# A written order of 1,867 steps, replaced by another one, in a fused HGRN2 attention and SERF MLP kernel

## The chip, the cores and the metric

The kernel runs on one core of one Trainium2 chip. The metric is the device time of one execution in microseconds (us). Engine names in the profile: PE is TensorE (PEld its weight loads), DVE is VectorE, ACT is ScalarE, POOL is GpSimd, SP is SyncE, which here issues most DMAs.

## The reference

Two functions in a row, q, k, v and the gate's logits as (4, 8, 768, 48), weights of 384 x 2048 and 2048 x 384:

```python
f = 1.0 / (1.0 + np.exp(-f_logit))
for t in range(S):
    state = f[:, :, t, :, None] * state + np.einsum('bhd,bhe->bhde', k[:, :, t], v[:, :, t])
    y[:, :, t] = np.einsum('bhd,bhde->bhe', q[:, :, t], state)
x = y.transpose(0, 2, 1, 3).reshape(B * S, H * D)     # 3072 x 384
h = x @ w_in
sp = np.maximum(h, 0.0) + np.log1p(np.exp(-np.abs(h)))
return (h * erf(sp)) @ w_out
```

The weights arrive as float64, two 32-bit words an element.

## The kernel before

**Tiling.** The 3072 tokens are 24 chunks of 128 (g = 0 to 23, each in two halves c of 64) and 12 blocks of 256 (blk). Attention goes by chunks, in the chunked form of the recurrence; the MLP goes by blocks and by four groups of 512 hidden columns (gi). The weights come in 16 pieces, 768 KB each as float64: 8 of w_in, 8 of w_out. VectorE and ACT turn a piece into fp32 in seven steps (`round_step`).

**Order.** The program is one list of tokens, STEPS. `run_steps` goes through it and each token issues its instructions at the end of the queues of its engines; the scheduler changes nothing (`manual_schedule`), so each engine executes its instructions in the order of the list, and waits where another engine's result or a free buffer is missing. A token reads `name numbers engine @ places`: `m4_0_1` is the mask of chunk 4, half 0, row group 1; `c1_3a@11` copies block 1, group 3 by ACT (a; v is VectorE) into slot 11. Places are 15 SBUF slots and the PSUM bank pairs 0 to 3.

The tokens that the text speaks of:

- f, q, k, v, p: loads of gate logits, queries, keys, values and a weight piece, by SP. r: a rounding step. cl, ex, ln, d, e: log decays (d on TensorE, "log sums"), qd, kd: queries and keys times decays (VectorE).
- tq, tk, tx: transposes of qd and kd (TensorE), aq, ak: their copies to SBUF (qA, kT).
- sc: *scores* (TensorE, L593), m: *mask* of the scores (VectorE, L618), four per chunk. ds: *state products* (TensorE, L581), to, ta: totals of the decays, st: state update (VectorE, L557/L558). y: attention rows (TensorE, L644), x/xa/xb/xt: their copies.
- h: hidden columns from plain fp32 (L686, blocks 0 to 2). hf, ht: hidden columns from three f32r parts (L705, blocks 3 to 11). c: copy of h. ae, ax, aw, at, au, ah, am: the activation on ACT and VectorE. ka, kb, kt: h in parts. o, oa, ot: output (L772), plain or by parts. nc, no: fetches of parts of w_out from DRAM, by POOL. ro, so, rh, sh: rows out. ck: the check on the decays, whose flag all engines read at the end. z: matmuls on constants that keep TensorE busy (L443).

Attention's matmuls use a part of TensorE's array (64 x 64 tiles and others), the MLP's the whole.

**One bank pair for three results.** Scores, state products and totals of a chunk lie in one bank pair, side by side, in a single tile:

```python
def scored(g, n=None):
    if g not in scs:
        scs[g] = bank_pair(n)
    t = scs[g]
    w = HP * C
    return (
        t[:, :, 0:w].rearrange("s r (a t) -> s r a t", t=C), t[:, :, w : w + HP * D],
        t[:, 0, w + HP * D : w + HP * D + 2 * HP],
    )
```

`mask` reads the first of them, `add_state` the second.

Of the kernel before, what the change touches and what calls it, by code (L numbers as in the profile page):

```python
# [47 lines left out]
def kernel(  # L82
# [760 lines left out]
    def pads(_):  # L843
# [60 lines left out]
        oa4_2 v12 no4_3@2 kt4_1 oa4_3 ak11a@6 aq11@9 o4_1_1_1 at4_3 nc4_4@7 o4_1_0_1 k12 aw4_3@4
        st20 sc11@3 nc4_5@14 ds11 m10_0_1 sp20a d13@0 st21 ot4_2 e13 m11_0_1 st22 y10_1@2 sp21a
        no4_4@5 m11_1_0 y10_0 sp22a td12 m11_1_1 ot4_3 w12 ms12 v13 xa10 m11_0_0 ka4_2@8@1
        y11_1@0 xb10 y11_0 kb4_2 oa4_4 xa11 w13 oa4_5 kt4_2 o4_2_1_1 o4_2_0_1 xb11 f19@8 xt11
        hf5_0@0 nc5_0@14 xt10 nc5_1@1 no4_5@7 au4_3 ht5_0 td13 hf5_4@2 qd12 ah4_3 f18 cl14 ht5_4
# [357 lines left out]
```

## Time and profile before

| | us |
|---|---|
| runs of the kernel | 569.91, 572.71, 574.5 (median 572.71) |
| the profiled execution: its span | 569.7 |
| TensorE busy | 550.9 (97%) |
| VectorE busy | 470.8 (83%) |
| ACT busy | 413.7 (73%) |
| POOL busy | 107.4 (19%) |

The mean granted clock of TensorE in the profiled execution is 0.994. The profile gives no time for the profiled execution beside its span, from the first to the last instruction. A row of the grouped view reads: line, engine, operation, output<-input, count | busy time, mean duration in ns | idle time of the engine ahead of it, and what ended most of it. A row of the timeline reads: start, duration, engine, line, operation, count. A plain fp32 matmul of the program is executed as two, so counts in the profile are twice those of the program there.

### The profile page before, as it was taken

Reading aid. Unit: us, or ns where it says so; the run is one execution under the profiler, and the core shown is the slowest. Engines: PE = TensorE matmul, PEld = TensorE weight load, DVE = VectorE, ACT = ScalarE, POOL = GpSimd, SP = SyncE. Lnnn points to the kernel's source line nnn. Section 1 sums busy time; section 2 is a strip of 40 time slices with the busy share of each in tenths; the row PEclk is TensorE's granted clock in tenths of the full one; section 3 lists DMA queues with packets and bytes.
Section 4 is the critical chain, followed back from the end, with each engine's and each line's share of the span. In section 5 each row is a group of like instructions: output and inputs, shape, how many; then the busy total and the mean of one; then the engine's idle time right before and its main releaser. Section 6 shows DMA issues by size and latency. Waiting matters only on the chain.

```text
span 569.7 us, 14855 instructions
## 1 busy us (share of the span) xinstructions
PE 550.9 (97%) x6175; PEld 462.7 (81%) x6175; DVE 470.8 (83%) x666; ACT 413.7 (73%) x513; POOL 107.4 (19%) x191
## 2 busy tenths in 40 slices
PE   8889999999999999999999999999999999999995
PEld 7768887756678668789979878989979989799983
DVE  5899999999988588987688999478888598695881
ACT  5877758799897575886986976588875766756860
POOL 1023003000030012014032124031215215110220
PEclk9999999999999999999999998999999999999998
DMA  8896785100563136389745889534887657552671
GB/s 192 214 282 149 218 221 159 56 0 0 108 145 65 23 91 217 130 195 250 138 116 148 214 193 248 121 63 137 216 186 201 175 161 204 121 140 61 172 217 62
DMA packets 155714, 85.59 MB, mean 150 GB/s; under 512 B 132244, under 2 KB 135316, under 8 KB 155640
## 3 DMA queue, kind: packets, MB, share of 16 engines
q1 hardware_dynamic: 139128, 42.68, 32.6%
q0 software_dynamic: 16512, 41.89, 26.2%
q8 instruction: 51, 0.84, 0.6%
q14 instruction: 23, 0.19, 0.1%
HBM read 73.41 MB, written 9.51 MB: 146 GB/s over the span
## 4 chain that ended last, share of the span: by engine, by line
PE 58%; DVE 18%; issue 9%; DMA 7%; ACT 5%; SPq 1%; POOL 1%; DVEq 0%; POOLq 0%; ACTq 0%
PE pair L772 25%; PE pair L705 18%; PE pair L686 5%; DVE e L181 4%; DMA piece<-form_dram 3%; PE pair L644 2%; PE pair L593 2%; PE pair L515 2%; PE pair L581 2%; DVE qA L618 1%; DMA raw_x<-in_moe_w_in_dram 1%; DMA out_dram<-rows 1%; DVE raw_y L351 1%; DVE plain_o L358 1%; PE pair L461 1%
## 5 line engine op out<-in xcount | busy, mean ns | idle before, releaser
L181 DVE SCALAR_TENSOR_TENSOR e<-x,e 128x1024 f32<-128x1024 f32 x96 | 116.8, 1220 | 35.4 <-ACT x L176 25.6
L176 ACT ACTIVATE x<-h,serf_bias 128x1024 f32<-128x1024 f32 x88 | 100.0, 1147 | 30.9 <-DVE e L181 14.1
L772 PE MATMUL pair<-plain_o,h 128*128 128x384 f32 x320 | 110.7, 492 | 0.0
L398 POOL DMA_DIRECT2D piece<-form_dram x96 | 52.2, 546 | 275.1 <-PE pair L772 175.4
L772 PEld LDWEIGHTS pair<-plain_o,h 128*128 128x128 f32 x320 | 58.5, 190 | 36.6 <-DVE h L740 0.9
L290 POOL DMA_DIRECT2D sv<-in_v_dram x84 | 53.7, 652 | 168.7 <-PE pair L644 139.1
L772 PE MATMUL pair<-piece,g 128*128 128x384 f32 x384 | 81.3, 349 | 1.5 <-DMA piece<-form_dram 1.2
L705 PE MATMUL pair<-xT,form_x 128*128 128x256 f32 x432 | 77.8, 288 | 0.0
L705 PE MATMUL pair<-xT,form_i 128*128 128x256 f32 x432 | 74.1, 279 | 0.0
L772 PEld LDWEIGHTS pair<-piece,g 128*128 128x128 f32 x384 | 66.7, 190 | 5.8 <-DMA piece<-form_dram 1.8
L736 ACT ACTIVATE e<-e 128x1024 f32<-128x1024 f32 x48 | 50.4, 1054 | 26.2 <-DVE e L181 25.8
L705 PEld LDWEIGHTS pair<-xT,form_x 128*128 128x128 f32 x432 | 62.4, 188 | 4.4 <-issue 0.8
L686 PE MATMUL pair<-xT,plain_i 128*128 128x256 f32 x288 | 64.8, 381 | 0.2 <-DVE plain_i L358 0.2
L705 PE MATMUL pair<-xT,form_y 128*128 128x256 f32 x432 | 61.6, 281 | 0.0
L686 PEld LDWEIGHTS pair<-xT,plain_i 128*128 128x128 f32 x288 | 54.1, 190 | 9.1 <-issue 0.6
L705 PEld LDWEIGHTS pair<-xT,form_i 128*128 128x128 f32 x432 | 60.9, 188 | 0.0
L740 DVE TENSOR_TENSOR h<-h,e 128x1024 f32<-128x1024 f32 x44 | 53.5, 1220 | 5.4 <-ACT e L736 5.3
L705 PEld LDWEIGHTS pair<-xT,form_y 128*128 128x128 f32 x432 | 56.0, 188 | 0.8
L173 ACT ACTIVATE e<-h 128x1024 f32<-128x1024 f32 x44 | 46.0, 1052 | 13.1 <-DVE h L137 5.7
L618 DVE TENSOR_TENSOR qA<-pair,tri 64x256 f32<-64x256 f32 x96 | 40.5, 422 | 7.0 <-PE pair L593 2.8
L772 PE MATMUL pair<-form_o,g 128*128 128x384 f32 x192 | 39.9, 342 | 0.0
L529 ACT COPY qA<-pair 64x512 f32<-64x512 f32 x48 | 27.8, 578 | 12.6 <-PE pair L515 9.0
(105 smaller groups left out, 766.0 us busy)
## 6 DMA issues: line engine op xcount, KB each, us to landing
piece<-form_dram POOLq DMA_DIRECT2D x96, 384.0 KB, 4.0
raw_y<-in_moe_w_out_dram SPq DMA_DIRECT2D x8, 768.0 KB, 4.5
kn<-in_k_dram SPq DMA_DIRECT2D x24, 192.0 KB, 3.0
vt<-in_v_dram SPq DMA_DIRECT2D x24, 192.0 KB, 4.1
qn<-in_q_dram SPq DMA_DIRECT2D x24, 192.0 KB, 4.0
form_dram<-piece SPq DMA_DIRECT2D x12, 384.0 KB, 3.4
out_dram<-rows SPq DMA_DIRECT2D x11, 384.0 KB, 3.4
sv<-in_v_dram POOLq DMA_DIRECT2D x84, 48.0 KB, 3.3
```

Of the source, the lines that this page charges most:

```text
L173: nc.scalar.activation(out=dst[:], in_=h, func=AF.Exp)
L176: nc.scalar.activation(out=dst[:], in_=h, func=AF.Tanh, bias=serf_bias[:, i : i + 1], scale=SERF_KAB[i][0])
L181: nc.vector.scalar_tensor_tensor(out=e[:], in0=x[:], scalar=SERF_KAB[i][2], in1=e[:], op0=ALU.add, op1=ALU.mult)
L290: nc.gpsimd.dma_start(out=svs[g % NSV][half(1 - r), r, c, :, PAD : PAD + D], in_=v[b, r::2, t0 : t0 + C, :].rearrange("a t d -> t a d"),)
L398: nc.gpsimd.dma_start(out=streams[i, blk, u], in_=form_dram[i, u])
L529: nc.scalar.copy(out=qAs[g][half(r), r].rearrange("p a (c t) -> p a c t", c=2), in_=ps[half(r)])
L618: nc.vector.tensor_tensor(out=to, in0=sc[half(c), r], in1=tri1[half(c)].unsqueeze(1).broadcast_to((C, HP, C)), op=ALU.mult,)
L686: nc.tensor.matmul(hts[blk, gi][:, 2 * i + j, :], lhsT=w[:, kt, j * P : (j + 1) * P], rhs=xTs[blk][:, 0, kt, :], start=(kt == 0), stop=(kt ...
L705: nc.tensor.matmul(hts[blk, gi][:, 2 * i + j, :], lhsT=w[:, kt, j * P : (j + 1) * P], rhs=x[:, kt, :], start=(blk, p) not in begun, stop=True,
L736: nc.scalar.activation(out=e[:], in_=e[:], func=AF.Tanh, scale=SERF_C)
L740: nc.vector.tensor_tensor(out=h, in0=h, in1=es.pop((blk, gi))[:], op=ALU.mult)
L772: nc.tensor.matmul(ots[blk][:, tt, 0:d_model], lhsT=lhs, rhs=rhs, start=("o", blk, tt) not in begun, stop=True, skip_group_check=True,)
```

## The change

STEPS is another list. Apart from the dummy matmuls (27 before, 20 after) it holds the same work, in another order, with other slots and bank pairs. Eleven copies of transposed keys (ak) go from VectorE to ACT, and some copies of hidden columns, states, rows and values change between the two; kernel lines move up by 34 to 36. Four helpers take their slots one at a time, and dummies always go to a bank pair that they name:

```diff
-    def out_c(u, n, n2):
-        streams[u] = [piece(m) for m in (n, n2)]
+    def out_c(u, n):
+        streams[u] = [piece(n)]
         take_c(streams[u][0], out_words(u))
+
+    def out_m(u, n):
+        streams[u].append(piece(n))
+        take_m(streams[u][1], streams[u][0], out_words(u))
...
-    def keep_busy(times, n=None):
-        to = busy[-1]
-        if n is not None:
-            ahead[n] = bank_pair(n)
-            to = ahead[n][:, 0, 0:P]
+    def keep_busy(times, n):
+        ahead[n] = bank_pair(n)
         for _ in range(times):
-            nc.tensor.matmul(to, lhsT=tri[:], rhs=tri[:], start=True, stop=True)
+            nc.tensor.matmul(ahead[n][:, 0, 0:P], lhsT=tri[:], rhs=tri[:], start=True, stop=True)
...
-    def part_a(blk, gi, n, n2):
-        gps_[blk, gi] = [slot(m, "g", F32R) for m in (n, n2)]
+    def part_a(blk, gi, n):
+        gps_[blk, gi] = [slot(n, "g", F32R)]
...
-    def part_b(blk, gi):
+    def part_b(blk, gi, n):
+        gps_[blk, gi].append(slot(n, "g", F32R))
...
-    def project(blk, gi, tt, *more):
+    def project(blk, gi, tt, n=None):
         whole = (blk, gi) not in gps_
-        rows_tile(blk, more[-1] if len(more) == (1 if whole else 2) else None)
+        rows_tile(blk, n)
...
     STEPS = """
-        f1@0 f0 k0 p0 zb0@0 in0 v0 cl1 q0 ex1 cl0 ex0 k1 ln0 z11 d0@1 e0 q1 kd0 r0_0 z4 to0@1 v1
...
+        f0@0 cl0 ex0 ln0 z12@0 d0@0 f1 cl1 ex1 ln1 z1@1 d1@1 ms0 in0 q0 v0 k0 q1 e0 z1@2 to0@2
+        v0_1_1v v0_1_0v e1 qd0 tq0@3 aq0@1 kd0 v1 k1 v0_0_1v v0_0_0v qd1 ta0 ds0 st0 st1 sp1v
...
```

**Chunk 4.** On TensorE, before, state products (L581) follow the scores (L593) of chunk 4 at once; its bank pair is pair_879:

```order
L515 MATMUL pair_836<-ident,kd_93 128x64 x8
L686 MATMUL pair_857<-xT,plain_i_519 128x256 x6
L593 MATMUL pair_879<-qA,kT 64x64 x16
L581 MATMUL pair_879<-vt_84,kd_93 64x48 x16
L686 MATMUL pair_919<-xT,plain_i_519 128x256 x12
```

In the changed kernel (scores now L558, state products L546, plain hidden columns L651) chunk 4 has pair_846 and chunk 5 pair_719:

```order
L651 MATMUL pair_851<-xT,plain_i_584 128x256 x6
L558 MATMUL pair_846<-qA,kT 64x64 x16
L558 MATMUL pair_719<-qA,kT 64x64 x16
L546 MATMUL pair_846<-vt_84,kd_93 64x48 x16
L546 MATMUL pair_719<-vt_85,kd_94 64x48 x8
L426 MATMUL pair_937<-lt,tri_60 64x192 x4
L651 MATMUL pair_851<-xT,plain_i_584 128x256 x6
```

On VectorE in the changed kernel, three masks of chunk 4 (L583) stand among rounding steps of weight piece 5 (plain_i_591), and in the list all three stand ahead of ds4:

```order
L572 COPY Tall<-pair_719 128x4x2
L583 TENSOR_TENSOR qA<-pair_846,tri_60 64x4x64 x2
L303 TENSOR_SCALAR plain_i_591<-plain_i_591 128x2x3x128
L572 COPY Tall<-pair_846 128x4x2
L308 SCALAR_TENSOR_TENSOR plain_i_591<-raw_y_605,plain_i_591 128x768
L312 TENSOR_SCALAR raw_y_605<-plain_i_591 128x2x3x128
L583 TENSOR_TENSOR qA<-pair_846,tri_60 64x4x64
L317 SCALAR_TENSOR_TENSOR raw_y_605<-raw_y_605 128x768
```

Before, all masks of a chunk stand behind its state products in the list. In the built program an instruction that touches a tile waits for the earlier ones of other engines that touch it, so state products of chunk 4 now wait for the third mask of these rows.

**Chunk 7.** On TensorE, before, state products come ahead of the scores (pair_1557):

```order
L772 MATMUL pair_1538<-plain_o_778,h 128x384 x4
L581 MATMUL pair_1557<-vt_85,kd_94 64x48 x16
L593 MATMUL pair_1557<-qA,kT 64x64 x16
L772 MATMUL pair_1295<-plain_o_1042,h 128x384 x4
```

In the changed kernel they come behind them (pair_1483):

```order
L738 MATMUL pair_1326<-plain_o_1293,h 128x384 x4
L558 MATMUL pair_1483<-qA,kT 64x64 x16
L546 MATMUL pair_1483<-vt_85,kd_94 64x48 x16
L426 MATMUL pair_1548<-lt,tri_60 64x192 x4
```

and on VectorE the three masks that stand ahead of ds7 in the list come behind rounding steps of a piece of w_out (plain_o_1354), two passes of the activation (e) and queries times decays (qd):

```order
L317 SCALAR_TENSOR_TENSOR raw_y_1359<-raw_y_1359 128x768
L324 TENSOR_TENSOR plain_o_1354<-raw_y_1359,plain_o_1354 128x768
L147 SCALAR_TENSOR_TENSOR e<-x,e 128x1024
L324 TENSOR_TENSOR plain_o_1354<-raw_y_1355,plain_o_1354 128x768
L449 TENSOR_TENSOR qd<-qn_88,dp_95 128x8x48
L147 SCALAR_TENSOR_TENSOR e<-x,e 128x1024
L583 TENSOR_TENSOR qA<-pair_1483,tri_60 64x4x64 x3
```

The masks moved ahead of the state products of the same chunk at these two places, and at chunks 13, 16, 18 and 23.

More of the change, by code (lines that the diff above doesn't have):

```diff
@@ L904 @@
[L904 to L908, printed above, removed]
-        ex14 hf5_1 kd12 ht5_1 ln14 am4_3 hf5_5 q14 c5_0a@4 tt12 ae5_0@11 hf5_2@0 aw5_0@9 hf5_3
@@ new lines @@
+        h0_5@2 r8_0 sp10a h0_4 c0_2a h1_5@1 h1_4 c1_2a@10 tx6@0 aq6@8 ak6a@13 y4_0@3 y4_1 y5_1@2
+        y5_0 x4a x5a r8_1 w7 w6 ds6@1 q8 td6 v7 p11 f9@1 k8 r9_2 au0_1 sc6 m6_1_1 m6_0_0 r8_2
+        r8_3 r9_3 m6_1_0 ah1_0 ax0_2@4 aw1_1@5 r11_0 r9_4 r9_5 v8 f8 tt6 k7 d7@0 e7 ah0_1
+        ae1_3@13 aw0_0@6 m6_0_1 au1_1 am1_0 r9_6 au0_0 r8_4 kd7 r11_1 r11_2 ax1_3@11 r11_3 r8_5
+        r11_4 r11_5 am0_1 cl8 r8_6 st12 h2_4@3 h2_2@2 h2_3 h2_6@0 h2_5 c2_1a@5 ah1_1 ah0_0
+        c2_2a@14 ae1_2@6 ae0_2@2 at0_2 r11_6 ex8 r10_5 st13 q7 p13 sp12a r13_0 h2_7 h2_1@2 at1_3
@@ new lines @@
+        am1_1 r10_6 qd7 r13_1 am0_0 r13_2 r13_3 h2_0 o1_0_1@3 o1_0_0 o1_1_0 o1_1_1 o0_1_1@1
+        o0_0_0 p12 p15 td7 tt7 p14 k9 aw1_3@4 r12_0 ln8 r15_0 r12_1 r13_4 r12_2 r13_5 r13_6
+        aw0_2@11 aw1_2@9 ax1_2@12 c2_0a@7 r14_0 c2_3a@3 au0_2 at1_2 r12_3 r15_1 r12_4 ms6 ah0_2
+        d8@2 ae2_2@11 e8 y6_1@0 y6_0 tx7@2 ak7a@12 o0_1_0 o0_0_1 r12_5 r15_2 r12_6 au1_2 am0_2
+        ah1_2 am1_2 o1_2_0 kci2 ae0_3@8 ax2_3@9 xa6 aq7@2 sc7@2 au1_3 kd8 r15_3 r14_1 r14_2
+        ah1_3 aw0_3@6 ax0_3@4 r15_4 xb6 r15_5 r14_3 am1_3 r14_4 r14_5 r14_6 at0_3 r15_6 sp13a
@@ new lines @@
+        kci0 qd8 au0_3 m7_0_1 m7_1_1 m7_1_0 ds7 kci1 ax2_2@12 d9@0 aw2_2@1 kci3 ae2_3@13 st14
+        st15 m7_0_0 at2_3 f11@4 td8 f10 o1_2_1 o0_2_1 ah0_3 am0_3 aw2_3@10 o0_2_0 kci5 sp14a e9
+        td9 v9 o1_3_0 o1_3_1 ro1a@6 ae2_1@9 ae2_0@0 so1 tt9 q10 tt8 k10 q9 au2_3 kMi0 kMi2 kMi1
+        cl10 kDi1 y7_0@2 y7_1 xa7 xb7 ah2_3 kci4 kDi0 kMi3 xt6 xt7 kDi3 tx8@0 o0_3_0 ax2_0@8
+        ex10 ln10 kco0@2 o0_3_1 kci7 ro0a@10 aw2_1@6 hf3_1@3 hf3_0 ht3_0 at2_2 kd9 qd9 kDi2
+        hf3_3@2 ht3_3 ht3_1 hf3_2 am2_3 o2_3_1@1 ht3_2 o2_3_0 aw2_0@12 at2_0 au2_0 au2_2
@@ new lines @@
+        sc10@0 ds10 td11 q12 k12 sCo4 q11 k11 tt10 sCo2 so0 ro2a@12 so2 w10 w11 d12@1 e12 kDi6
+        kDi5 hf3_5 xb8 hf4_1@3 hf3_4 ht3_7@1 xt8 kDi7 hf3_7 ht4_1 m10_1_0 m10_0_1 ae3_0@7 at3_0
+        m10_1_1 ht3_6 ah3_1 kd11 c3_2v@9 sp19a aw3_2@10 ax3_2@14 qd11 st20 am3_1 kd12 hf3_6
+        ht4_0 m10_0_0 au3_0 st21 sp21v sp20a y10_1@2 y10_0 c3_3a@12 ae3_2@11 at3_2 kMo2@0 au3_2
+        k13 sCo3 v12 td12 q13 tt12 v11 ah3_0 ah3_2 xa10 tx11@1 am3_0 sMo2 kMo3@3 sMo3 k14 tt11
+        ae3_3@14 kco1@10 o3_1_1@0 hf4_0 o3_1_0 am3_2 kDo3 xb10 kco5@7 qd12 ax3_3@11 at3_3
@@ new lines @@
+        nc4_2@4 st27 ax4_1@0 aw4_1@9 ae4_1@2 c5_0v@13 sp26 td15 q15 td14 tt14 tx14@3 ak14a@7
+        aq14@8 y12_0@2 y12_1 xa12 at4_1 kd15 au4_1 y13_1@1 y13_0 xa13 xb13 xb12 ae5_1@14 aw5_1@0
+        at5_1 au5_1 ah4_1 am4_1 aw5_0@10 ah5_1 am5_1 sc14@3 ds14 nc4_3@7 w14 no5_3@9 ot4_0
+        ht5_7@1 hf5_5@2 ht5_5 o4_3_0 ka4_1@6 oa4_2 m14_1_1 kb4_1@5 kt4_1 oa4_3 ht5_6 o4_1_0
+        hf5_7 o4_1_1 no4_1@0 no4_3@2 ot4_3 ot4_1 no4_2@14 ka5_1@4 kb5_1@7 st28 qd15 m14_1_0
+        ax5_0@6 ae5_0@5 kt5_1 m14_0_0 at5_0 hf5_4 ht5_4 c5_2a@2 ae5_2@0 ax5_2@3 au5_0 aw5_2@6
@@ new lines @@
+        ah5_0 hf5_6 ot4_2 o4_3_1 nc5_3@10 no5_2@1 nc5_2@14 q17 sp27 st29 m14_0_1 k16 sp28
+        y14_1@2 tt15 q16 ro4a@11 y14_0 xa14 c5_3a@8 at5_2 xt12 f16@3 k17 so4 f17 v15 sp29 tx15@3
+        ot5_3@0 oa5_3 o5_1_0 hf6_3@1 xt13 am5_0 xb14 au5_2 ax5_3@5 ka5_0@9 kb5_0@10 ah5_2 am5_2
+        kt5_0 ae5_3@6 aw5_3@11 at5_3 au5_3 aq15@0 ka5_2@5 ht6_1@2 oa5_2 o5_1_1 ht6_0 ht6_2 w16
+        hf6_0 hf6_2 ot5_2 kb5_2@4 o5_2_1 o5_0_0 nc5_4@14 oa5_4 ht6_3 ah5_3 xt14 no5_1@7 ot5_1
+        w15 nc5_0@11 hf6_1 o5_2_0 nc5_1@1 no5_4@12 no5_0@14 kt5_2 am5_3 cl16 oa5_0 ex16 ln16
@@ new lines @@
+        ak15a@6 c6_1v@7 c6_0a@4 aw6_0@11 sc15@1 ds15 m15_0_1 st30 st31 d16@3 d17@2 sp30 f18@6
+        ot5_0 ot5_4 o5_0_1 oa5_1 e16 e17 kd17 kd16 qd16 m15_1_1 m15_1_0 o5_3_0 y15_1@3 m15_0_0
+        y15_0 tx16@2 ae6_0@3 ax6_0@13 at6_0 ae6_1@14 ax6_1@12 at6_1 aw6_1@10 au6_1 o5_3_1
+        ht6_4@1 hf6_4 ht6_5 no5_5@1 nc6_3@9 nc5_5@0 ot5_5 oa5_5 hf6_5 nc6_0@13 nc6_2@12 aq16@10
+        ah6_1 au6_0 ah6_0 ak16a@8 q18 k18 td16 f19 am6_1 ka6_1@11 am6_0 xa15 ka6_0@14 oa6_3@2
+        kb6_1@1 o6_1_1 ro5v@2 c6_2a@3 aw6_2@0 kt6_1 qd17 cl18 kb6_0@5 xb15 ht6_6@0 v16 k19 tt16
@@ new lines @@
+        so5 td17 sp31 o6_1_0 oa6_2 hf6_7 sc16@1 m16_0_1 ds16 m16_0_0 kt6_0 st32 st33 tx17@3
+        m16_1_0 tt17 v17 sp32 o6_0_1 ht6_7 oa6_0 o6_0_0 nc6_1@9 oa6_1 hf6_6 ex18 ae6_2@1 ln18
+        ax6_2@11 at6_2 m16_1_1 xt15 aq17@12 ak17a@2 sc17@3 c6_3a@8 ds17 m17_0_0 au6_2 m17_1_1
+        st34 m17_0_1 d18@1 ax6_3@13 e18 ae6_3@5 at6_3 ah6_2 am6_2 kd18 qd18 aw6_3@9 au6_3 ah6_3
+        m17_1_0 am6_3 ht7_2@0 no6_0@14 no6_1@11 w17 no6_3@2 no6_2@0 hf7_3 ht7_1@1 ht7_0 ot6_0
+        ht7_3 hf7_2 c7_1v@13 hf7_1 ot6_1 tx18@3 ak18a@14 aq18@1 hf7_0 c7_0a@9 ax7_0@4 ot6_2
@@ new lines @@
+        sc18@0 m18_1_0 m18_0_0 td18 sp34 q19 sp33 v18 v19 tt18 ds18 m18_1_1 st36 st37 ot6_3
+        y17_1@3 m18_0_1 k20 f21@11 f20 ae7_0@5 at7_0 ax7_1@0 y16_0@1 y17_0 aw7_1@14 xa17 ms18
+        xb17 y16_1 ae7_1@2 d19@0 e19 o6_3_1 ht7_6@3 o6_3_0 ht7_4@0 kd19 xa16 xb16 qd19 cl20
+        ka6_2@7 ex20 ln20 at7_1 au7_1 kb6_2@12 kt6_2 nc6_4@10 tx19@1 oa6_4 hf7_7 hf7_6 w18
+        no6_5@6 no6_4@4 ot6_4 ht7_7 no7_2@0 nc6_5@8 oa6_5 ot6_5 ah7_1 am7_1 aw7_0@14 au7_0
+        aq19@10 c7_3v@2 ah7_0 am7_0 ka7_1@4 ht7_5 o6_2_0 o6_2_1 kb7_1@14 xt16 ak19a@7 ro6a@8
@@ new lines @@
+        au10_0 ah9_3 ah10_0 am10_0 ka10_0@12 aw10_2@0 at10_2 au10_2 kb10_0@8 ht11_1@0 ot9_4
+        hf10_3 ot9_5 hf10_6 ht10_2 c10_1v@7 ax10_1@9 nc10_0@14 no9_2@10 nc10_4@5 no10_2@0 ht11_0
+        hf10_7 ht10_7 hf11_0 ck0 o10_0_0@1 oa10_1 o10_0_1 oa10_0 ot9_2 am9_3 o9_3_1 o9_3_0
+        ae10_1@2 ah10_2 at10_1 c10_3v@4 am10_2 ka10_2@14 oa10_4 nc10_3@9 kb10_2@3 o10_2_0
+        o10_2_1 ht11_7@2 ht11_6 nc10_5@10 aw10_1@13 ro9a@11 so9 au10_1 ah10_1 am10_1 ax10_3@13
+        ae10_3@5 at10_3 ka10_1@2 kb10_1@11 ht11_2@3 ht11_3 oa10_5 hf11_1 c11_0a@13 ax11_0@10
@@ new lines @@
+        kt10_2 kt10_1 kt10_0 ae11_0@3 oa10_3 o10_1_1 ht11_4@0 ot10_2 hf11_2 o10_1_0 hf11_3
+        no10_5@14 ot10_5 no10_3@9 ot10_3 hf11_6 hf11_7 nc10_2@8 oa10_2 no10_4@12 ot10_4 hf11_4
+        aw11_0@0 at11_0 au11_0 aw10_3@10 ah11_0 au10_3 ah10_3 am11_0 am10_3 no10_0@11 ka11_0@0
+        kb11_0@10 c11_1v@14 ae11_1@7 aw11_1@9 ot10_0 nc11_0@3 oa11_0@3 no11_0@5 no10_1@2
+        nc11_1@8 c11_3v@6 ax11_3@12 kt11_0 ot11_0 ax11_1@11 at11_1 au11_1 aw11_3@3 ae11_3@5
+        at11_3 au11_3 ht11_5 hf11_5 c11_2a@11 aw11_2@9 ah11_3 am11_3 ah11_1 am11_1 oa11_1 ot10_1
@@ L989 @@
+        o10_3_0 o10_3_1 ro10v@0 so10 o11_3_0 no11_1@8 nc11_2@1 ot11_1 ax11_2@2 nc11_5@12
+        nc11_3@3 ka11_1@5 ae11_2@4 kb11_1@7 o11_1_1 o11_0_1 oa11_3 oa11_2 o11_3_1 o11_1_0 at11_2
+        au11_2 ah11_2 am11_2 kt11_1 ka11_2@8 kb11_2@13 kt11_2 no11_2@2 ot11_2 o11_2_1 oa11_5
+        no11_3@0 no11_5@9 ot11_5 nc11_4@3 ot11_3 oa11_4 no11_4@1 ot11_4 rh11_1v@4 sh11_1 o11_2_0
+        o11_0_0 rh11_0a sh11_0 ck1@2 ck2
     """.split()
@@ L992, in run_steps @@
         do = {
-            "z": keep_busy, "zb": lambda _, n: busy.append(bank_pair(n)[:, 0, 0:P]), "f": load_f, "p": load_piece, "r": round_step, "w": load_sv, "in": pads,
+            "z": keep_busy, "f": load_f, "p": load_piece, "r": round_step, "w": load_sv, "in": pads,
             "q": lambda g: load(g, q, qns[g % NQ]), "k": lambda g: load(g, k, kns[g % NQ]), "v": load_v,
@@ L1005, in run_steps @@
             "nc": fetch_form(0), "no": fetch_form(1), "oa": project_form(0), "ot": project_form(1),
-            "kco": out_c, "kMo": lambda u: take_m(streams[u][1], streams[u][0], out_words(u)),
+            "kco": out_c, "kMo": out_m,
             "kDo": out_d, "sCo": keep_form(0), "sMo": keep_form(1),
```

197 lines of the change are left out of this document (64 added, 133 removed).

## The prediction

> **What bounds the kernel now.** I read the page first (busy time, the slices), then the stretches of 20 us, then TensorE's and VectorE's own rows, and last the waits.
>
> ```profile
> span 569.7 us, 14855 instructions
> PE 550.9 (97%) x6175; PEld 462.7 (81%) x6175; DVE 470.8 (83%) x666; ACT 413.7 (73%) x513; POOL 107.4 (19%) x191
> 0.00:20.00 20.00, 16.02 (x212) 14.27 (x212) 13.53 (x33) 12.93 (x27) 1.74 (x11) 1.00 0.89 204
> 20.00:40.00 20.00, 17.78 (x367) 14.11 (x358) 17.67 (x41) 15.14 (x34) 3.33 (x5) 1.00 0.98 266
> 40.00:60.00 20.00, 18.85 (x176) 16.26 (x175) 19.89 (x32) 16.01 (x19) 5.99 (x7) 1.00 0.64 142
> 100.00:120.00 20.00, 20.00 (x82) 15.16 (x81) 20.00 (x24) 16.29 (x18) 0.00 (x0) 1.00 0.13 40
> 120.00:140.00 20.00, 19.66 (x65) 11.92 (x64) 20.00 (x22) 19.87 (x21) 0.00 (x0) 1.00 0.00 0
> 340.00:360.00 20.00, 18.42 (x257) 16.34 (x256) 15.45 (x25) 10.39 (x16) 7.61 (x14) 0.91 1.03 235
> ```
>
> The columns behind the length are busy time of PE, PEld, DVE, ACT, POOL, then granted clock, DMA share and GB/s. TensorE is busy 97% of the whole, but that is an average of two regimes. From 40 to 140 us VectorE has no gap either (19.89 to 20.00 of 20 in the rows shown): it turns the float64 weights into fp32 (the rounding steps), and TensorE keeps pace with it. Afterwards (row 340) VectorE has slack and TensorE alone sets the pace. So the first 140 us are decided by how the two queues interlock, the rest by TensorE's work and its few waits.
>
> A busy TensorE hides its losses, because ends of matmuls are modelled. So I count work from start to start.
>
> ```profile
> 43.60 18.37 PE L686 MATMUL pair<-xT,plain_i 128*128 128x256 f32 x84 [0.20 <-DVE plain_i L358]
> 61.90 0.88 PE L461 MATMUL pair<-lt,tri 64*64 64x192 f32 x16
> 62.71 2.86 PE L686 MATMUL pair<-xT,plain_i 128*128 128x256 f32 x12
> 65.50 0.47 PE L515 MATMUL pair<-ident,qd 64*128 64x64 f32 x8
> 65.80 0.41 PE L515 MATMUL pair<-ident,kd 64*128 64x64 f32 x8
> 66.14 2.86 PE L686 MATMUL pair<-xT,plain_i 128*128 128x256 f32 x12
> 68.93 0.69 PE L593 MATMUL pair<-qA,kT 48*64 48x64 f32 x32
> 69.44 0.63 PE L581 MATMUL pair<-vt,kd 64*64 64x48 f32 x32
> 70.01 5.45 PE L686 MATMUL pair<-xT,plain_i 128*128 128x256 f32 x24
> 86.94 2.01 PE L644 MATMUL pair<-qA,sv 128*32 128x64 f32 x128
> 88.88 5.43 PE L772 MATMUL pair<-plain_o,h_x 128*128 128x384 f32 x16
> 94.14 6.21 PE L686 MATMUL pair<-xT,plain_i 128*128 128x256 f32 x28
> ```
>
> ```profile
> 394.90 0.86 PE L772 MATMUL pair<-piece,g 128*128 128x384 f32 x4
> 395.60 0.87 PE L705 MATMUL pair<-xT,form_y 128*128 128x256 f32 x6
> 397.71 0.52 PE L705 MATMUL pair<-xT,form_x 128*128 128x256 f32 x3
> 398.06 0.52 PE L705 MATMUL pair<-xT,form_i 128*128 128x256 f32 x3
> ```
>
> A plain hidden record takes (61.90 - 43.60) / 84 = .218 us (a plain fp32 matmul is two records), scores .51 / 32 = .016, state products .57 / 32 = .018, attention rows 1.94 / 128 = .015, transposes .34 / 8 = .043, log sums .81 / 16 = .05, plain output 5.26 / 16 = .329 (the mean over the whole trace is .31), output by parts .70 / 4 = .175, hidden by parts .35 / 3 = .118.
>
> ```profile
> 101.45 0.54 DVE L333 TENSOR_SCALAR plain_o<-plain_o 128x768 f32<-128x768 f32 x1
> 101.92 0.94 DVE L351 SCALAR_TENSOR_TENSOR raw_y<-raw_y 128x768 f32<-128x768 uint32 x1
> 102.79 1.21 DVE L740 TENSOR_TENSOR h_x<-h_x,e 128x1024 f32<-128x1024 f32 x1
> 103.92 0.94 DVE L358 TENSOR_TENSOR plain_o<-raw_y,plain_o 128x768 f32<-128x768 f32 x1
> L618 DVE TENSOR_TENSOR qA<-pair,tri 64x256 f32<-64x256 f32 x96 | 40.5, 422 | 7.0 <-PE pair L593 2.8 <-PE pair L581 2.5
> ```
>
> VectorE likewise, start to start: one-input rounding step .47, two-input step .87, a pass over 1024 columns 1.13 to 1.14, a mask .42. The mask's row also says that masks (L618) waited 2.5 us for *state products* (L581), which they do not read: the two share a bank pair, and the program orders whoever touches it.
>
> **The change, part by part.** *Changes between whole-array and part tiles.* In the built order 46 excursions into part tiles stand where 65 stood. One costs about .2: 12 hidden records between two excursions take 2.79, against 12 x .218 = 2.61. 19 x .2 is about 4 us of TensorE, all on its path from 140 us on. Without that saving the sum below is 4 higher (rival C). Seven dummy matmuls fewer (27 to 20) lie in waits of the start and give nothing.
>
> *Fetches.* Two visible waits on form pieces go, since the new list asks earlier:
>
> ```profile
> PE pair L772 <- DMA piece<-form_dram: 1.2, 2, 1.0
> PEld pair L772 <- DMA piece<-form_dram: 1.8, 2, 1.2
> ```
>
> I credit 1.6, between these rows' 1.2 and 1.8.
>
> *Engines.* Eleven kT copies go to ACT, other copies change sides: VectorE's work falls by some 11 us, ACT's rises by 8. VectorE is saturated only before 140 us, where few of these lie.
>
> *The new wait.* In six chunks (4, 7, 13, 16, 18, 23) state products now stand behind masks of the same chunk; before, none did. Two of them lie where VectorE is saturated. State products of chunk 4 are matmuls after 54.9 us of TensorE's work, but wait for a mask that ends after 58.6 us of VectorE's. I count VectorE's list to there: 22 two-input steps 19.3, 24 one-input 11.6, 19 masks 8.0, 12 decays 5.6, 15 state updates 4.7, the rest 9.4. VectorE's own idle time comes on top. Before, it is 6.5 in the first 20 us and 2.3 in the next (20 - 13.53, 20 - 17.67). The new list loads gates, queries and values ahead of the weights, so I take 5.5, bounds 4 and 8.9. TensorE then stands at 58.6 + 5.5 = **64.1**. Queued behind it is everything on TensorE: its own loss so far would be about 4, so 5 us are new.
>
> Next, mask 6 on VectorE waits for scores 6. From state products 4, TensorE has 84 plain hidden records 18.2, attention rows 2.0, state products and scores 1.8, transposes and log sums 1.1: **23.1**. VectorE has 16.0 in the same stretch, so it goes idle for 7.1 us with its rounding queued behind the mask.
>
> Then state products 7, after 46.6 us more of TensorE, wait for three masks. VectorE has 23 two-input steps 20.0, 18 one-input 8.4, 17 wide passes 19.4, 7 masks 3.0, the rest 4.2: **55.0**. TensorE waits 8.4 us. So the path crosses over three times, each time to the engine with more in hand.
>
> *Clock.* The trace has one stretch at half clock:
>
> ```profile
> 349.24 0.21 PE L515 MATMUL pair<-ident,qd 64*128 64x64 f32 x1 [1.28 <-issue]
> 351.02 2.81 PE L772 MATMUL pair<-piece,g 128*128 128x384 f32 x8
> 353.62 1.31 PE L772 MATMUL pair<-form_o,g 128*128 128x384 f32 x4
> 354.77 0.52 PE L705 MATMUL pair<-xT,form_x 128*128 128x256 f32 x3
> ```
>
> After a wait of 1.28, twelve matmuls took 3.75 where 12 x .175 is 2.1: 1.65 lost (the row 340:360 says .91 of 20, 1.8). I take 1.4 behind each of the two long waits, bounds 0 and 3.4, as part of the slow time may fall into the wait. The Trainium skill ("TensorE: Matmul & The Clock Gate", What's actually happening) lets the clock fall to half after an idle window of about 3.4 us and rise again after a busy window as long. By it both long waits bring half clock, an estimate of up to 1.7 lost behind each, and the sum would be .6 higher at most; the wait of 1.28 above, shorter than its window, would have brought none, and there the trace disagrees.
>
> *The other four chunks*, where VectorE has slack: scores, one to three masks of .42, at 23 also a copy of 1.1 ahead, then state products: .7 to 2 us each, 5 together. Scores 9 and 11 now stand behind state updates of the same pair (.36 each for two steps and more): 1.5. At the end the copy of one half of the last rows stands ahead of the other half's last matmuls: .8. With small change, 7.5; bounds 5 and 10.
>
> *TensorE's rest* after state products 7: 312 plain output records 96.6 (at .31), 576 by parts 101.7, 1296 hidden by parts 153.3, attention rows 17.4, scores and state products 16.6, transposes 10.3, log sums 6.4: **402.4**.
>
> *What is lost anyway.* The same counting for before leaves 16.3 us between 162 and 563.2: six single waits of 4.9 (1.2 of them the fetches), half clock 1.4, and 10 in many small hand-overs. I keep 10 (8.5 to 11) and 1 for clock.
>
> *The end.*
>
> ```profile
> 561.75 1.45 PE L772 MATMUL pair<-plain_o,h 128*128 128x384 f32 x4
> 563.24 0.56 DVE L137 COPY rows<-pair 128x384 f32<-128x384 f32 x1 [6.26 <-PE pair L772]
> 563.82 0.90 SPq L816 DMA_DIRECT2D out_dram<-rows  x2
> 563.88 0.48 ACT L137 COPY rows<-pair 128x384 f32<-128x384 f32 x1 [8.16 <-DVE rows L137]
> ```
>
> From 563.2 to 569.7 are 6.5. After, one of the copies is done earlier (-.5), but the last steps of the check on the decays now come last: 6.8.
>
> *Sum:* 64.1 + 23.1 + 1.4 + .4 (scores and first mask) + 55.0 = 144.0 at state products 7; + 1.4 + 402.4 + 10 + 7.5 + 1 + 6.8 = **573.1**, against the profiled 569.7: **+3.4**. The median of the runs shown, 572.71, lies 3.0 above that span (the lowest, 569.91, .2 above). So I say **576**.
>
> **The rivals.**
> *A, faster: the masks hold nobody up.* For it: it needs no more than VectorE being earlier, or the waits being met. Then TensorE's list of 124.6 + 402.4 = 527.0, some 4 lost early, 2.3 at mask 6, 10 + 2.3 + 1 and 6.8 give 553.4, a run of 556. If only VectorE's own list binds (129.6 + 5.5 = 135.1 at state products 7, no idle time at mask 6), 564.2, a run of 567. Against: TensorE executes in order, and the built program has these waits.
>
> *B, slower: VectorE is late by ACT too.* In the third stretch ten of the 17 wide passes are e<-x,e, which need ACT's terms:
>
> ```profile
> L181 DVE SCALAR_TENSOR_TENSOR e<-x,e 128x1024 f32<-128x1024 f32 x96 | 116.8, 1220 | 35.4 <-ACT x L176 25.6 <-ACT e L173 8.9
> ```
>
> 35.4 / 96 is .37 each, 3.7 for ten; all of it is on the path, because TensorE already waits for VectorE there. It decides from the point where ACT delivers later than VectorE arrives. With it 576.8, a run of 580; with the high start (8.9 idle) 583. Against: the row 100:140 had no idle VectorE.
>
> *C, the saving isn't there:* excursions cost only what the neighbours give back; then 4 us come back, a run of 580. Against: the 2.79 above, for a gap of its own.
>
> **How the numbers follow.** Forecast .50 (own range 569 to 582), A .28 (two thirds at 556 to 562, the rest near 567), B .14, C .08. Within 1% (567.0 to 578.4, about what a measurement here can tell from no change): .42, nearly all of it the forecast's. Faster by more: .27. Slower by more: .31 (B, C, and the upper part of the forecast, where the start is late or w is 10). Range 558 to 585: down into A, up to B with a late start; each end leaves about a tenth.
>
> **What would show it.** State products of chunk 4 starting near 64 us with an idle TensorE of about 5 ahead, released by VectorE's mask; VectorE idle for 7 us ahead of a mask near 80 to 88; TensorE idle for about 8 near 144; half clock in the two stretches behind; no wait on form pieces above .3; some 4 us less from start to start over the rest. I am wrong if these three waits are short: then the time is A's. I am wrong upward if further waits of several us show behind ACT between 90 and 144.

## The result, and the profile after

The changed kernel takes 589.67 us (median of four runs, 587.21 to 591.0), against 573.61 of the kernel before in the same runs: a ratio of 1.0295, interval 1.0238 to 1.0352. It is slower by 16 us; forecast were 3.4, in a range that ended at 585. Here and below a median takes in every run, while a ratio leaves out runs far above the rest of the same kernel (of the kernel before one of 577.52, of the last two versions one each, of 2779.56 and 1892.95).

The profiled execution has a span of 589.3 us. Page and stretches of 20 us, columns as before:

```profile
span 589.3 us, 14768 instructions
PE 551.1 (94%) x6161; PEld 466.7 (79%) x6161; DVE 464.0 (79%) x652; ACT 417.6 (71%) x525; POOL 106.1 (18%) x191
0.00:20.00 20.00, 16.02 (x232) 13.57 (x232) 14.35 (x42) 12.47 (x27) 1.74 (x11) 1.00 0.91 198
20.00:40.00 20.00, 17.47 (x293) 14.77 (x293) 16.36 (x33) 13.53 (x29) 2.72 (x4) 0.83 0.95 234
40.00:60.00 20.00, 20.00 (x246) 16.81 (x245) 18.05 (x30) 15.37 (x21) 5.22 (x8) 1.00 0.70 184
60.00:80.00 20.00, 14.53 (x167) 12.09 (x166) 14.91 (x24) 9.72 (x13) 0.00 (x0) 0.83 0.41 126
140.00:160.00 20.00, 10.41 (x94) 6.17 (x93) 17.22 (x26) 13.19 (x17) 0.00 (x0) 0.74 0.14 24
```

The same two late stretches of the kernel before:

```profile
60.00:80.00 20.00, 20.00 (x197) 16.93 (x196) 19.45 (x33) 12.64 (x17) 0.00 (x0) 1.00 0.80 221
140.00:160.00 20.00, 20.00 (x238) 11.98 (x240) 18.93 (x34) 17.70 (x26) 0.00 (x0) 1.00 0.53 100
```

In both, TensorE had no gap before, and VectorE next to none in the first. Now TensorE, VectorE and ACT all lose time in 60 to 80, and TensorE is busy half of the time in 140 to 160. What TensorE waited for (total, times, longest; the largest rows, and the one for form pieces):

```profile
PE pair L546 <- DVE qA L583: 16.1, 6, 9.6
PE pair L558 <- DVE state L522: 3.0, 2, 1.7
PE pair L558 <- DVE Tall L572: 2.7, 1, 2.7
PE pair L546 <- DVE Tall L572: 1.8, 1, 1.8
...
PE pair L738 <- DMA piece<-form_dram: 0.2, 1, 0.2
```

The first row is the forecast mechanism: state products (L546) wait for masks (L583), six times, once per chunk that was named. TensorE's timeline at chunks 4 and 7:

```profile
65.48 0.69 PE L558 MATMUL pair<-qA,kT 48*64 48x64 f32 x32
68.88 0.69 PE L558 MATMUL pair<-qA,kT 48*64 48x64 f32 x32 [2.70 <-DVE Tall L572]
72.34 1.83 PE L546 MATMUL pair<-vt,kd 64*64 64x48 f32 x45 [2.77 <-DVE qA L583]
...
145.27 0.69 PE L558 MATMUL pair<-qA,kT 48*64 48x64 f32 x32
155.56 1.11 PE L546 MATMUL pair<-vt,kd 64*64 64x48 f32 x32 [9.59 <-DVE qA L583]
```

State products 4 start at 72.3 and not at 64.1, and scores 5 had already waited 2.7 for a copy of totals out of their pair, which the sum did not have. State products 7 start at 155.6, not at 144.0. What happens on ACT and VectorE behind the first wait:

```profile
65.36 0.94 ACT L297 ACTIVATE plain_i<-raw_y 128x768 f32<-128x768 f32 x1
75.03 0.49 ACT L435 ACTIVATE dp<-pair 128x384 f32<-128x384 f32 x1 [8.74 <-PE pair L426]
```

```profile
71.87 0.42 DVE L583 TENSOR_TENSOR qA<-pair,tri 64x256 f32<-64x256 f32 x1
72.32 0.96 DVE L317 SCALAR_TENSOR_TENSOR raw_y<-raw_y 128x768 f32<-128x768 uint32 x1
73.31 0.96 DVE L324 TENSOR_TENSOR plain_i<-raw_y,plain_i 128x768 f32<-128x768 f32 x1
75.94 0.56 DVE L456 TENSOR_TENSOR kd<-kn,kd 128x384 f32<-128x384 f32 x1 [1.67 <-ACT kd L435]
...
81.09 0.56 DVE L299 TENSOR_SCALAR plain_o<-plain_o 128x768 f32<-128x768 f32 x1 [4.26 <-ACT plain_o L297]
...
87.31 1.23 DVE L147 SCALAR_TENSOR_TENSOR e<-x,e 128x1024 f32<-128x1024 f32 x1 [2.35 <-ACT e L139]
...
98.48 0.86 DVE L583 TENSOR_TENSOR qA<-pair,tri 64x256 f32<-64x256 f32 x2 [1.07 <-PE pair L558]
```

TensorE's wait holds the log sums (L426) of chunk 6, these hold ACT for 8.7 us, and ACT holds VectorE three times, 8.3 us together. Only 1.07 is left of the wait that the prediction had put ahead of mask 6.

### The profile page after: what moved, and what is told of

Same layout as the page of the kernel before. It is cut to its first block, busy times and chain, and to the rows that moved or that the text cites. A ratio compares the mean times of both kernels' runs of the same rounds, so it can differ in the third digit from the quotient of the medians.

```text
span 589.3 us, 14768 instructions
## 1 busy us (share of the span) xinstructions
PE 551.1 (94%) x6161; PEld 466.7 (79%) x6161; DVE 464.0 (79%) x652; ACT 417.6 (71%) x525; POOL 106.1 (18%) x191
## 4 chain that ended last, share of the span: by engine, by line
PE 70%; DVE 15%; DMA 5%; ACT 4%; SPq 3%; issue 3%; POOL 0%; DVEq 0%; ACTq 0%; POOLq 0%
PE pair L738 33%; PE pair L670 23%; DVE e L147 3%; PE pair L609 3%; PE pair L651 2%; PE pair L546 2%; DMA lt<-in_f_logit_dram 2%; PE pair L480 2%; DMA kn<-in_k_dram 2%; SPq L235 2%; PE pair L558 2%; DVE raw_y L317 1%; DVE qA L583 1%; PE pair L426 1%; DVE plain_o L324 1%
## 5 line engine op out<-in xcount | busy, mean ns | idle before, releaser
L142 ACT ACTIVATE x<-h,serf_bias 128x1024 f32<-128x1024 f32 x88 | 98.3, 1143 | 18.5 <-PE pair L426 6.5
L256 POOL DMA_DIRECT2D sv<-in_v_dram x84 | 52.4, 638 | 247.1 <-PE pair L609 208.4
L738 PEld LDWEIGHTS pair<-plain_o,h 128*128 128x128 f32 x320 | 60.3, 193 | 38.9 <-issue 3.5
L670 PE MATMUL pair<-xT,form_x 128*128 128x256 f32 x432 | 76.1, 284 | 0.0
L738 PEld LDWEIGHTS pair<-piece,g 128*128 128x128 f32 x384 | 65.3, 188 | 3.9 <-DMA piece<-form_dram 0.9
L651 PE MATMUL pair<-xT,plain_i 128*128 128x256 f32 x288 | 67.4, 395 | 0.0
L651 PEld LDWEIGHTS pair<-xT,plain_i 128*128 128x128 f32 x288 | 56.5, 199 | 9.2 <-issue 0.8
L103 ACT COPY h<-pair 128x1024 f32<-128x1024 f32 x30 | 30.3, 1009 | 34.5 <-PE pair L670 26.0
L583 DVE TENSOR_TENSOR qA<-pair,tri 64x256 f32<-64x256 f32 x96 | 40.4, 421 | 16.7 <-PE pair L558 7.8
```

Source lines behind the costliest of these rows:

```text
L103: (engine.copy if engine is nc.scalar else engine.tensor_copy)(out=out, in_=in_)
L142: nc.scalar.activation(out=dst[:], in_=h, func=AF.Tanh, bias=serf_bias[:, i : i + 1], scale=SERF_KAB[i][0])
L256: nc.gpsimd.dma_start(out=svs[g % NSV][half(1 - r), r, c, :, PAD : PAD + D], in_=v[b, r::2, t0 : t0 + C, :].rearrange("a t d -> t a d"),)
L583: nc.vector.tensor_tensor(out=to, in0=sc[half(c), r], in1=tri1[half(c)].unsqueeze(1).broadcast_to((C, HP, C)), op=ALU.mult,)
L651: nc.tensor.matmul(hts[blk, gi][:, 2 * i + j, :], lhsT=w[:, kt, j * P : (j + 1) * P], rhs=xTs[blk][:, 0, kt, :], start=(kt == 0), stop=(kt ...
L670: nc.tensor.matmul(hts[blk, gi][:, 2 * i + j, :], lhsT=w[:, kt, j * P : (j + 1) * P], rhs=x[:, kt, :], start=(blk, p) not in begun, stop=True,
```

## The experiments

All edit the list of steps; times are medians, with the ratio to the kernel before in the same runs. The kernel before took 573.61 us in the result's runs and 571.2 to 572.5 in those below, and the changed kernel was timed in the result's runs alone. So a difference from the changed kernel is taken from the two ratios, at 571.4 us for the kernel before, and one of less than some 4 us lies within the intervals. Positions come from one profile each. Profiles of kernels that are edited behind 34 us differ there by 1 to 1.5 us already, as the first stretch at half clock does not fall at the same time in each.

**State products of chunk 4 (and 5) early.** `... sc4 ds4 sc5 ds5 m4_0_1 m4_1_1 r5_2 ta4 r5_3 r5_4 m4_0_0 ...`

> The changed kernel with state products of chunks 4 and 5 issued right behind their scores, ahead of the masks. Theory M (the mask holds TensorE, and behind TensorE the decays of chunk 6, so ACT and VectorE starve too): the wait of 2.8 us at state products 4 goes, the wait of 2.7 at scores 5 (for the copy of the totals) stays, and the kernel gains 3 to 6 us, about 585. Rival V (VectorE is late anyway and sets the pace up to 140 us): no more than 1 us, 588 to 590.

584.67 us, ratio 1.0247 (1.0213 to 1.0281): 2.7 less than the changed kernel, between the two forecasts, and the intervals overlap, so the time alone does not decide. State products 7 stand 5.5 us earlier, at 150.1; 1.3 of this was there ahead of the edit. That is Theory M's mechanism. In this profile, the slowest of the five runs, 1.1 us of the lead are lost in a stretch at half clock at 280 us.

**State products of chunk 7 early.** `sc7@2 ds7 au1_3 ...` in place of `... m7_0_1 m7_1_1 m7_1_0 ds7`.

> The changed kernel with state products of chunk 7 issued right behind their scores, ahead of the masks. Theory M: the wait of 9.6 us and the half clock around it (2 us) go, gain 9 to 12 us, 577 to 580. Rival V: TensorE only reaches its next need of VectorE earlier and waits there, gain of 4 us at most, 585 or more.

576.41, ratio 1.0119 (1.0068 to 1.017): 10 less, within the 9 to 12 of Theory M and far from the rival's 4. The wait at chunk 7 is not covered by anything.

**Dummies in the waits.** `z8@3` ahead of sc5, `z8@3` ahead of ds4, `z27@0` ahead of ds7.

> The changed kernel with dummy matmuls in three waits: 8 ahead of scores 5, 8 ahead of state products 4, 27 ahead of state products 7 (about 2.6, 2.6 and 8.9 us of work, no longer than the waits). Theory C (the idle time is what halves the clock, and the slow stretches behind the waits cost 2.9 and 2.2 us): full clock from 34 to 245 us, gain 4 to 6 us, 583 to 586. Rival: the clock falls for another reason, or what runs slow is covered by waits: no change, 588 to 591.

590.97, ratio 1.0371 (1.0321 to 1.042): no gain, rather a loss. The clock stayed full from 32 to 97 us, but TensorE, now 3.6 us ahead of the changed kernel, then stopped for 3.8 us in the middle of scores 6, and behind the stop ran at half clock for 6.8 us; after both it was 2.7 us behind. To have the same without the wait at chunk 7, the kernel with state products 7 early got `z8@3` ahead of sc5 and of ds4:

> The kernel with only state products 7 early, and 8 dummy matmuls each in the waits ahead of scores 5 and of state products 4 (2.6 us each, no longer than the waits). Theory C (half clock from 67 to 77 us is on the path): full clock there and a gain of 3 us, 573 to 574. Rival: at full clock TensorE only arrives earlier at scores 6 and waits there for ACT: 576 to 577.

577.91, ratio 1.0119 (1.0073 to 1.0165), that of the same kernel without dummies. The time is the rival's, but its reason is not what happened: TensorE did not wait for ACT. TensorE's timeline at scores 6, and the transfers of 94 to 99 us by queue (packets, MB, share of 16 engines; the first three rows):

```profile
93.92 0.58 PE L558 MATMUL pair<-qA,kT 48*64 48x64 f32 x25
98.44 0.34 PE L558 MATMUL pair<-qA,kT 48*64 48x64 f32 x7 [3.93 <-issue]
```

```profile
q1 hardware_dynamic: 3128, 1.04, 95.0%
q0 software_dynamic: 145, 0.23, 19.1%
q8 instruction: 1, 0.02, 1.3%
```

"issue" means that no wait is on record; the stop lies inside one step. TensorE was 2.3 us ahead of the kernel without dummies, 1.9 behind it after the stop, and 3.2 behind after 3.4 us at half clock that follow. Instructions are being loaded (q8) while other transfers fill the DMA engines; but the changed kernel's page counts 50 such loads in an execution, so one beside the stop shows little. The cause is open, and so is whether full clock without a stop would have been worth time.

**All six early,** `ta4` and `ta5` (copies of totals) right behind their matmuls, `v18` ahead of scores 18:

```diff
-        ... sc13@2 m13_0_0 m13_0_1 ds13 ...
+        ... sc13@2 ds13 m13_0_0 m13_0_1 ...
```

> The changed kernel with all six state products (chunks 4, 7, 13, 16, 18, 23; 5 too) right behind their scores, the copies of totals 4 and 5 right behind the totals, and values 18 loaded ahead of scores 18. Theory M: about 20 us less of waits and half clock, 567 to 573, level with the kernel before or a little under it. Rival V: half of it comes back as other waits for VectorE, 577 to 582.

567.47, ratio 0.9928 (0.9896 to 0.996): 21 us less than the changed kernel, and slightly faster than the kernel before. Theory M: what the change cost is these waits and what they drew after them. The edit also moves the copy of totals that scores 5 waited 2.7 us for; how much of the 21 is that one is not separated.

**The waits put into the kernel before.** In its list state products 4 and the hidden columns behind them were moved behind three masks, so that the orders of TensorE and of VectorE stay as they were:

```diff
-        ... sc4@2 ax0_1@10 f9 ds4 m4_1_0 h0_7@0 qd5 r8_4 m4_0_0 r10_1 k7 m4_1_1 q7 r10_2 ...
+        ... sc4@2 ax0_1@10 f9 m4_1_0 qd5 r8_4 m4_0_0 r10_1 k7 m4_1_1 q7 ds4 h0_7@0 r10_2 ...
```

> The kernel before the change, with state products of chunk 4 (and the hidden columns behind them, so that TensorE's and VectorE's own orders stay word for word) behind three masks of chunk 4 in the list. Scores 4 end at 69.5 us there, the third mask would end near 73. Theory M: a wait of about 3.4 us on TensorE, and the time 2 to 4 us longer than before, since TensorE and VectorE run in step up to 160 us. Rival V: within 1 us of before.

577.47, ratio 1.0115 (1.0081 to 1.0148). The wait is the expected one:

```profile
74.28 0.68 PE L581 MATMUL pair<-vt,kd 64*64 64x48 f32 x32 [3.28 <-DVE qA L618]
```

and it reaches the end: TensorE stood 1.1 us behind the kernel before at 44 us, ahead of the edit, 4.8 from state products 4 on, and 4.6 at the end (spans 574.3 and 569.7). By the ratio of the runs the kernel is 6.6 us slower (4.6 to 8.5), more than the 2 to 4 expected; where the rest comes from is not shown. The order of masks and state products costs by itself, in either list, with each engine's own order untouched.

**The price of a change of tiles.** The kernel with six early, with 24 dummies `z1` between two part-tile steps, and with 24 between two whole-array steps:

> The kernel with the six state products early, and 24 single dummy matmuls of the whole array put between two steps in part tiles, all behind 190 us. A dummy takes .33, so 7.9 us in any place. If a change of tiles costs about .2 for there and back, 24 more of them cost 3 to 5 us beyond the same dummies put among whole-array steps (the other run): 578 to 581 against 575. If it costs nothing beyond that, both read the same.

> The kernel with the six state products early, and the same 24 dummy matmuls put between two steps of the whole array, behind 190 us: no change of tiles added. 7.9 us on the path: about 575.

575.15, ratio 1.006 (1.0031 to 1.0088), and 570.35, ratio 0.9987 (0.995 to 1.0024). The difference is 4.8 us for 24, .20 each (4.2 by the ratios, 5.1 in the spans, 575.4 and 570.3). Neither time is the expected one (578 to 581, and 575), because a dummy does not cost .33 in any place. One of each, as TensorE's timeline shows them (a dummy is the row L408, two records; first between part-tile steps, then between whole-array ones):

```profile
195.96 0.49 PE L408 MATMUL pair<-tri 128*128 128x128 f32 x2
196.38 0.82 PE L609 MATMUL pair<-qA,sv 128*32 128x64 f32 x44
...
201.71 0.38 PE L408 MATMUL pair<-tri 128*128 128x128 f32 x2
201.85 0.60 PE L670 MATMUL pair<-xT,form_x 128*128 128x256 f32 x3
```

From the dummy's start to the next step's start it is .42 between part-tile steps (most of the 24 have .42 to .62) and .14 between whole-array steps (19 of 24). Over all 24 the two sums are 11.6 and 4.8: a difference of 6.8 us on TensorE, .28 each, of which 4 to 5 arrive in the runs.

**Scores 9 and 11** right behind their state products and copies, ahead of `st18` and `st22`:

> The kernel with the six state products early, and scores 9 and 11 ahead of the state updates that read their pair. Theory M: waits of 1.6 and 1.9 us and the half clock behind the second (1.7) go, 562 to 564. Rival: they come back at the next need of VectorE, 566 to 568.

565.81, ratio 0.9869 (0.9804 to 0.9934), against 0.9928 without. The time lies between the two forecasts and the intervals overlap: undecided. The profile has neither wait and no half clock there, but more of it early, at 17, 27 and 68 us.

**Why VectorE came late to chunk 4.** First two copies of totals, `ta2` right behind `to2@1`, `ta4` behind `m4_1_1`, in the kernel with six early:

> The kernel with the six state products early, and two copies of totals on VectorE at other places: that of chunk 2 right behind its matmuls (it stood behind a piece's seven rounding steps, and state products 2 waited 1.1 to 1.5 us for it at 26 us), that of chunk 4 behind its masks again (scores 4 waited 2.0 for it). Theory T (the lateness of VectorE and TensorE at the start comes from copies of totals that hold a bank pair): 3 to 4 us of waits go, 563 to 565. Rival D (VectorE's lateness at the start comes from loads and from ACT, and these waits only show it): within 1 us of 567.

564.88, ratio 0.9882 (0.9812 to 0.9951): some 2.6 less, as Theory T had it, but the intervals again overlap. Then `ta2` alone, in the changed kernel:

> The changed kernel with one copy moved: that of the totals of chunk 2 stands right behind its matmuls and not behind seven rounding steps. Theory T (this copy makes state products 2, scores 2 and their masks late, 2.2 us on VectorE and a stretch at half clock on TensorE at 27 us): gain of 2 to 4 us, 585 to 587. Rival D (loads and ACT set the start): within 1 us of 589.

590.23, ratio 1.0309 (1.0263 to 1.0355): nothing in the time, though state products 7 stand at 152.7, 2.9 earlier. Theory T's 2 to 4 us do not show in the time. So nine two-input rounding steps were left out, which leaves those weights rounded incompletely:

> The changed kernel with nine two-input rounding steps of pieces 2, 3, 4, 6 and 7 left out (so these weights are rounded incompletely): 7.8 us less on VectorE ahead of the masks of chunk 4, as if it had come there with the idle time that the prediction took. Theory S (that term of the sum was the error, and the rest holds): state products 4 near 66 us, where TensorE's own loss then binds, state products 7 near 147 instead of 155.6, 579 to 582 in all. Rival: VectorE's lateness hardly matters, since ACT and the loads give the pace: 586 or more.

588.61, ratio 1.0273 (1.0224 to 1.0322): 1.3 less, within the noise. Of the 7.8 us, 3.1 arrive at state products 4 (69.2) and 3.4 at state products 7 (152.2). VectorE waited for ACT in place of working:

```profile
55.07 0.56 DVE L299 TENSOR_SCALAR plain_i<-plain_i 128x768 f32<-128x768 f32 x1 [3.81 <-ACT plain_i L297]
65.01 0.56 DVE L299 TENSOR_SCALAR plain_i<-plain_i 128x768 f32<-128x768 f32 x1 [2.39 <-ACT plain_i L297]
```

These are second rounding steps of a piece. The first is done by ACT, which in this profile works without a gap from 49.8 to 65 us, so VectorE came there before ACT could. And the lead that did arrive was lost later. TensorE kept 3 to 4 us of it up to chunk 13, where a stretch at half clock took most of it within 6 us; the changed kernel passes the same steps at full clock. The changed kernel, then this one:

```profile
284.90 1.68 PE L738 MATMUL pair<-piece,g 128*128 128x384 f32 x8
286.42 0.87 PE L670 MATMUL pair<-xT,form_y 128*128 128x256 f32 x6
...
282.57 2.93 PE L738 MATMUL pair<-piece,g 128*128 128x384 f32 x8
285.29 1.45 PE L670 MATMUL pair<-xT,form_y 128*128 128x256 f32 x6
```

The run with `ta2` alone lost its 2.4 to 3.7 us in the same place and the same way. So "nothing" in these two times does not show that nothing was gained at the start. The control, the same steps left out of the kernel before:

> The kernel before with the same nine steps left out, as a control. If VectorE's lateness costs the changed kernel more than the kernel before, because there three waits hang on it, the gain here is well below that of the other run: 0 to 4 us, 567 to 571. If the steps are worth the same in both lists: 8 us, 563.

569.24, ratio 0.9956 (0.9921 to 0.9991): 2.5 less, so the steps are not worth more in the changed list. Theory S falls, by the positions and not by the time alone: state products 4 and 7 should have stood near 66 and 147, and stood at 69.2 and 152.2. VectorE's own work does not carry the missing time. Last, ACT's three steps ahead of the decays that wait (`ae0_0@7 ae1_1@9 r10_0 e6`):

> The changed kernel with three steps of ACT (two exponentials of hidden columns and the first rounding step of piece 10) ahead of the decays of chunk 6, which wait for log sums queued behind state products 4 on TensorE. Theory A (ACT's 8.7 us of idle time behind that wait starve VectorE, and so make the masks of chunk 7 late): state products 7 some 4 us earlier, gain of 3 to 5 us, 584 to 586. Rival: VectorE waits for something else at once, 588 to 590.

589.68, ratio 1.0281 (1.0217 to 1.0346): nothing, as the rival had it. VectorE's wait of 4.3 for a rounding step became one of 3.4 of a state update for the copy of the state that ACT makes. State products 7 stand at 154.0, 1.6 earlier, but 1.1 of this was there ahead of the edit. In the changed kernel, helping one engine alone brought no time that the runs can tell; taking away the waits that couple them did.

**All together:** six state products early, scores 9 and 11, `ta2` and `ta5` early.

> The version with all that was found: the changed list with six state products right behind their scores, scores 9 and 11 ahead of the state updates, and the copies of totals 2, 4 and 5 moved. Theory M and T together: waits of about 22 us less than the changed kernel, some 4 us less than the best so far: 559 to 563, against 571 before. Rival: the moves overlap, 564 to 566.

559.05, ratio 0.9771 (0.9736 to 0.9806), a version that beats both. Once more, beside a version with `z4@3` ahead of `y0_0@3` and `z3@3` ahead of `to3@3`:

> The best version so far once more, beside the next run: 558 to 560.

> The best version with 4 dummy matmuls (1.3 us) ahead of attention rows 0, which wait 1.35 us at 18 us, and 3 (1.0 us) ahead of the totals of chunk 3, which wait .9 at 25 us. Theory C (these waits halve the clock from 26 to 32 us, and the 2.4 us that this costs TensorE are on the path): no slow stretch at the start, 556 to 557. Rival: what full clock gives there comes back as a wait for VectorE, 558 to 560.

559.61, ratio 0.9778 (0.9748 to 0.9808), and 561.37, ratio 0.9794 (0.9758 to 0.983): no gain from the dummies. The slow stretch at the start shrank to 3.4 us, and TensorE stood 1.2 us earlier at 60 us than in its partner; then it stopped at 89 us, again without a wait on record:

```profile
88.13 0.92 PE L651 MATMUL pair<-xT,plain_i 128*128 128x256 f32 x3
91.33 2.07 PE L651 MATMUL pair<-xT,plain_i 128*128 128x256 f32 x4 [2.29 <-issue]
```

The stop left it 1.1 us behind its partner, and 3.4 us at half clock right behind the stop 2.3 behind, which stayed to the end (spans 560.9 and 558.8).

## Why the prediction was wrong, point by point

The sum against the profile of the changed kernel:

| stretch | predicted | measured |
|---|---|---|
| start to state products 4 | 64.1 | 72.3 |
| to the first mask of chunk 6 | 24.9 | 26.1 |
| to state products 7 | 55.0 | 57.1 |
| to the last output matmul's end | 422.3 | 427.0 |
| the end | 6.8 | 6.7 |
| sum | 573.1 | 589.3 |

- **The waits: right** in place and number, and nearly in size: the first pair 2.7 + 2.8 (5 foreseen, all at state products 4), chunk 7 9.6 (8.4), the other four 1.2, .5, 1.0 and 1.0, 3.7 together (5). Taking them away brought 21 us. The 2.7 at scores 5, for a copy of totals, were in no term of the sum.
- **The step that failed: "so I take 5.5".** State products 4 came at 72.3, so what VectorE lost beside the counted 58.6 was 13.7 and not 5.5: 8.2 us too little, half of the 16.2 by which the sum is short. By the profile 11.4 of the 13.7 are idle time; the other 2.3 are steps that took longer than counted, as a step that directly follows the one it needs starts about .1 later (.59 from start to start at 59.25 us, where .47 was counted). The nearest rows of before gave 8.8 of idle time, and I went below them for an argument on loads that no row bore out. Two of the waits that the ledger did not have, for scores 2 behind a late copy of totals, and for a rounding step by ACT:

```profile
29.07 0.43 DVE L583 TENSOR_TENSOR qA<-pair,tri 64x256 f32<-64x256 f32 x1 [2.11 <-PE pair L558]
56.37 0.56 DVE L299 TENSOR_SCALAR plain_i<-plain_i 128x768 f32<-128x768 f32 x1 [1.54 <-ACT plain_i L297]
```

What set the rest of VectorE's idle time at the start stays open. The runs also show that this term is no cause that can be removed alone: with 7.8 us less work VectorE waited 6.2 for ACT.
- **"VectorE goes idle for 7.1 us" was right, the reason was not:** it waited for ACT, and ACT for log sums queued behind the waiting state products. I asked what is queued behind the wait and wrote "everything on TensorE", without following it to the engine that needs it first. Rival B named the mechanism, for a later stretch and at 3.7 us.
- **Clock: too small.** Four stretches at half clock (6.8, 6.8, 10.2 and 3.4 us long) cost TensorE some 3, 3, 2 and 1 us from start to start in its profile, against 3.8 in the sum. How much of this was on the path is open. Three times dummies took away or shortened a slow stretch and no time came, but each time a stop and another slow stretch followed; and the two runs that lost their lead at chunk 13 lost it at half clock.
- **The rest behind state products 7** is 4.7 longer than foreseen. Scores 9 and 11 waited 1.4 and 1.7, with half clock behind the second, where I had 1.5 for both.
- **Right:** .2 for a change of tiles (.20 in the pair of runs, .28 on TensorE itself); the fetches (1.2 became .2); the copy of half the rows at the end (.65 of .8); the end itself. A small slip: .35 / 3 is .117 and not .118, but .118 is what rows of the changed kernel give (2.12 / 18), so nothing hangs on it. The step from span to run was 3.0 in the forecast and 1.7 in the profiled execution.
- **Rival A** had the right way out: without the held masks the list is faster than before. It gave 556, or 567 with VectorE's list binding; the runs reached 567.5, and 559 with other waits taken away. **Rival C** falls: a change of tiles does have its price.

## What to carry to other kernels

In this program results that share a tile also share their waits: let the writers of neighbouring results come ahead of the first reader of any of them, above all where that reader's engine is saturated. Price a wait not by itself but by the first instruction behind it that another in-order engine needs, and follow it once round until it comes back. Where the rows of before give a lateness, a reordered list starts at that figure; going below it needs a row.
